# GpSimd's subtractions and products moved to VectorE in two stages, and a first score after 13 instead of 19 maximum units, in a fused attention, FFN and expert kernel

## The chip, the cores and the metric

The kernel runs on one core of a Trainium2 chip. A core has five engines that run side by side, each through its own queue in order: TensorE (PE, matrix multiply; PEld is its weight load), VectorE (DVE), ScalarE (ACT), GpSimd (POOL) and SyncE (SP, which here only issues DMAs). Engines wait for one another through semaphores. The metric is the device time of one execution in microseconds (us), the median of three runs.

## What is computed

Three stages, one after the other, all in 32-bit floats at the interface:

```python
# attention: q, k, v are (4, 8, 1152, 64); queries are averaged in pairs, so 576 queries
q_pool = q.reshape(B, H, S // 2, 2, D).mean(axis=3)
scores = q_pool @ k.T / sqrt(D)
attn = exp(scores - max(scores)); attn /= attn.sum() + 1e-9
x = attn @ v                       # 2304 tokens x 512
# dense FFN, w_in 512 x 2048, w_out 2048 x 512, given as 64-bit floats
h = x @ w_in;  x = (h * sigmoid(1.702 * h)) @ w_out
# experts: 8 experts, each token with a positive skip score goes to one
y = gate * (relu(x @ w1[e]) @ w2[e]);  out = x + y   # else out = x
```

## The kernel before, in words

Precision is kept by splitting each 32-bit operand of a matmul into a high part (F32R, written by a ScalarE copy) and a low part (operand minus high part), and by adding three products: high x high, low x high, high x low. Making low parts is elementwise work, and the change is largely about which engine does it.

**Attention** (`attention`) works on 16 pairs of heads; the two heads of a pair sit on partitions 0 to 63 and 64 to 127. A pair has 14 score units (`score_unit`): nine of 320 queries against 128 keys, then five of 256 queries against 256 or 128 keys. A unit's PSUM holds key x query scores, so the maximum of a query can't be subtracted per partition. Instead a fourth product adds it: `ONE` times `M2`, where row 0 and row 32 of each half of `M2` hold minus the maximum's high part `mh` and low part `ml`. So before a pair's first score can be finished, its maxima must be known: `max_unit` multiplies 128 queries by 384 keys at a time (two heads per unit, 14 units, 27 reductions by VectorE on line 230), `max_rows` takes the maximum over the three key parts, and `max_rows_put` transposes the result on TensorE, splits it and writes the rows into `M2` by small DMAs, all issued by SP. The loop runs in steps `g`; at step `g` it puts out score unit `g` and maximum unit `g + LEAD`, with `LEAD = 19`, so that 19 maximum units precede the first score unit. Loads, splits and sums of the following pairs hang on fixed steps (`BESIDE`, `start`, an agenda `ag`). VectorE, ScalarE and TensorE each run their list in the order in which the loop puts it out. Score tiles (`ss`) have two buffers, maximum tiles (`xs`, `mt`) three.

**FFN** (`ffn`): tokens come in chunks `CH` of 768, 384, 256, 256, 256 and 384, in pieces of at most 384, and the hidden dimension in 16 blocks `fb`. A step is one block and one piece: 12 matmuls of layer 1 into `h` (line 563, two buffers), `sigmoid` on ScalarE, product `g` on VectorE (569), high part `gh` on ScalarE, low part `gl` (572), and two steps later 9 matmuls of layer 2. In chunk 0, 32 steps long, each step also turns one 512-column piece of the 64-bit weights (`wr`) into two 32-bit parts with integer operations (`wsplit`): on VectorE a mask that drops the sign (450), a shift of the low word (451), a maximum (452), a shift-and-or (440), a shift-and-mask (454), an or (455) and a sign mask (444); ScalarE scales `t1` (441) and writes the high part (446); GpSimd multiplies the low part (445). The list `fq` holds these operations, and each step takes three ahead of `gl` and four behind it (`fill`). `put`, the high part of a piece, stands one step later in ScalarE's list, behind that step's line 441. The matmuls of block `fb` wait for the `wih` that `put` writes. GpSimd also makes `gl` in chunk 0 and multiplies the next chunk's tokens by their reciprocal sums (`xnorm`, 469).

**Experts** (`experts`): one slot for each expert that has tokens. A slot's tiles of 128 tokens run `tokens_tile`: `up` for the two halves of the hidden layer (24 matmuls, 922), relu of the first half on ScalarE (941) and of the second on VectorE (947), transposes (926), high and low parts `hT` (928, 929), `down` (24 matmuls, 937) and the result `yo` (957). Beside a slot's first tile the next expert's weights are split: 16 pieces (`splits`), high parts on ScalarE (800), low parts (801) on VectorE, every third (`q % 3 == 2`, five of 16) on GpSimd. They are put in lots of 3, 2, 2, 2 and 7 between the tile's own operations. As a stage buffer is released SP loads the weights of the expert after that (`weights`, eight DMAs of 512 KB). GpSimd also gathers token rows and scatters results by indirect DMAs.

Of the kernel before, what the change touches and what calls it, by code (L numbers as in the profile page):

```python
# [19 lines left out]
P = 128  # L20
# [51 lines left out]
class Kernel:  # L72
# [51 lines left out]
    def attention(self, ctx):  # L124
# [88 lines left out]
        def max_unit(p, i):  # L213
# [5 lines left out]
            if i < 12:  # L219
                part, t = divmod(i, 4)  # L220
                of = [(4 * u + t, part, d["qh"][HALF[u], t * P:t * P + P], d["kh"][HALF[u]]) for u in range(2)]
            else:
                of = [(8, part, BD[p % 2], d["kh"]) for part in ((0, 1), (2,))[i - 12]]
# [14 lines left out]
        def max_rows_put(p, m9):  # L238
# [6 lines left out]
            for row, m in ((0, mh), (32, ml)):  # L245
                for u in range(2):
                    r = slice(64 * u + row, 64 * u + row + 1)
                    dma(M2[p % 2][r, 0:512].rearrange("a (t q) -> a t q", q=P), m[4 * u:4 * u + 4])
                    dma(M2[p % 2][r, 512:], m[8:9, HALF[u]])
# [79 lines left out]
        LEAD = 19  # L329
# [35 lines left out]
        for g in range(-LEAD, NU * N + 20):  # L365
# [4 lines left out]
            px, ix = divmod(g + LEAD, NU)  # L370
            if 0 <= px < N:
                max_unit(px, ix)
                if ix == NU - 1:
                    max_rows(px)
# [9 lines left out]
            for f, *of in start.get(g + LEAD, ()):  # L384
                f(*of)
# [3 lines left out]
            if g == -LEAD + 12:  # L389
# [32 lines left out]
    def wsplit(self, fq, a, tmp, fb, k, ag=None):  # L422
# [20 lines left out]
        def last():  # L443
            V.tensor_scalar(sg, t2, 0xFF800000, None, op0=ALU.bitwise_and)
            (nc.gpsimd if fb else V).tensor_tensor(lo_t, t1.bitcast(F32), sg.bitcast(F32), op=ALU.mult)
            put = lambda: nc.scalar.activation(hi_t, t2.bitcast(F32), AF.Copy)  # L446
            put() if ag is None else ag.at(ag.now + 1, put)

        fq += [
            lambda: V.tensor_scalar(t2, hi, 0x7FFFFFFF, None, op0=ALU.bitwise_and),  # L450
            lambda: V.tensor_scalar(t1, hi, 23, None, op0=ALU.logical_shift_left),
            lambda: V.tensor_scalar(t2.bitcast(F32), t2.bitcast(F32), least, None, op0=ALU.max),
            low,
# [17 lines left out]
    def xtile(self, c, j, pc):  # L471
        i = (j * 2 + pc) if len(pieces(CH[c])) == 2 else (j * 2 + c % 2)
# [11 lines left out]
    def ffn(self, ctx):  # L484
# [60 lines left out]
        def xnorm(c, j, pc):  # L545
            xa[c, j, pc] = xr.tile([P, 384], F32, name="xa", tag="xa", bufs=4)
            self.xnorm(xa[c, j, pc], xraw.pop((c, j, pc)), c, j, pc, nc.gpsimd)
# [7 lines left out]
        def layer1(c, fb, pc, fa, fb_):  # L555
# [16 lines left out]
            (nc.gpsimd if c == 0 else V).tensor_tensor(gl, g, gh, op=ALU.subtract)  # L572
# [150 lines left out]
        for g in range(len(steps) + LAG):  # L723
            ag.now = g
            if g < len(steps):
# [11 lines left out]
                if fb == 0 and pc == 0 and c + 1 < len(CH):  # L737
                    for j in range(ND):
                        for q in range(len(pieces(CH[c + 1]))):
                            g0 = first[0, 10] + 2 * j if c == 0 else first[c, 4] + 2 * j  # L740
                            ag.at(g0, xload, c + 1, j, q)
                            ag.at(g0 + 1, xnorm, c + 1, j, q)
                            ag.at(first[c, NF - 1] + 1 if c == 0 else g0 + 4, xsplit, c + 1, j, q)
# [54 lines left out]
    def expert_split(self, s, q, raw, eng):  # L798
        hi, lo = self.piece(s, q)
        self.nc.scalar.activation(hi, raw, AF.Copy)  # L800
        eng.tensor_tensor(lo, raw, hi, op=ALU.subtract)  # L801
# [249 lines left out]
```

## Time and profile before

| | |
|---|---|
| median of 3 runs | 1119.11 us (1115.97 to 1127.57) |
| the profiled execution | 1114.21 us, of which its span, first to last instruction, is 1112.4 us |
| TensorE busy | 1017.9 us (91%) |
| VectorE busy | 806.9 us (73%) |
| GpSimd busy | 581.1 us (52%) |
| ScalarE busy | 482.1 us (43%) |
| granted TensorE clock, mean | 0.966 of 2.4 GHz |

A share over the whole span hides that the stages have different limits, so the stretches matter more: attention to 446 us, FFN chunk 0 to about 625 us, the other chunks to 912 us, experts to the end. In a timeline, a row is one instruction or a run of equal ones (`x27`): start, duration, engine, line, operation, output<-inputs; a bracket tells how long the engine had been idle and what ended that. Where two rows of one engine start closer together than the first one's duration, its pipeline overlaps them: the pace is read from start to start. The granted clock has two levels, 1.2 GHz (0.5) and 2.4 GHz (1.0); a mean between them is a mixture.

### The profile page before, as it was taken

To read this page: it belongs to the slowest core of one execution; us is meant where nothing else is said; L and a number is where in the kernel's file an instruction comes from. 1 tells how busy PE (TensorE), PEld (TensorE's weight loads), DVE (VectorE), ACT (ScalarE), POOL (GpSimd) and SP (SyncE) were. 2 spreads that over 40 slices of the span, in tenths; PEclk is the share of its full clock that TensorE was granted. 3 is DMA by queue.
4 is the path that set the end of the run, shared out by engine and by line. 5 is a ranking of instruction groups with operands and counts; after the bars stand their busy time and mean duration, and the time that the engine had idled before them with its cause. 6 is when DMAs were issued, how large, how long until landed. Compare 5 with 4: busy or idle time off the path is not lost. (4 is left out here: it accounts for less than half of the span.)

```text
span 1112.4 us, 19158 instructions
## 1 busy us (share of the span) xinstructions
PE 1017.9 (91%) x7002; PEld 801.3 (72%) x7002; DVE 806.9 (73%) x1584; ACT 482.1 (43%) x885; POOL 581.1 (52%) x408
## 2 busy tenths in 40 slices
PE   6999999999999999688978999999999989977893
PEld 4766767666776666587867898888889877755672
DVE  6767787778877772699999589787567555578734
ACT  2555555555555545243333332333332334256432
POOL 3698888998999988444445202101110106156413
PEclk9999999999999999889999999999999989988897
DMA  4233332223333210332333420211211326456301
GB/s 154 66 95 80 92 108 77 76 90 91 92 108 93 71 48 27 125 96 95 105 117 100 143 77 20 69 62 31 66 41 55 111 92 215 149 184 214 112 31 39
DMA packets 64325, 103.39 MB, mean 93 GB/s; under 512 B 18630, under 2 KB 34630, under 8 KB 64072
## 3 DMA queue, kind: packets, MB, share of 16 engines
q1 hardware_dynamic: 60148, 96.35, 27.4%
q0 software_dynamic: 3904, 5.15, 1.5%
q8 instruction: 69, 1.13, 0.4%
q14 instruction: 56, 0.46, 0.1%
q10 hardware_dynamic: 148, 0.30, 0.1%
HBM read 90.04 MB, written 17.35 MB: 97 GB/s over the span
## 5 line engine op out<-in xcount | busy, mean ns | idle before, releaser
L230 DVE TENSOR_REDUCE mx<-xs 128x1 f32<-128x384 f32 x432 | 213.0, 549 | 79.5 <-PE xs L227 74.8
L271 ACT ACTIVATE E<-ss 128x640 f32<-128x640 f32 (+1 forms) x224 | 174.0, 786 | 155.3 <-PE ss L270 123.0
L286 POOL TENSOR_TENSOR acc<-acc,E 128x640 f32<-128x640 f32 (+1 forms) x96 | 182.1, 1897 | 19.5 <-ACT E L271 15.4
L563 PE MATMUL h<-xh,wih 128*128 128x384 f32 (+1 forms) x448 | 145.8, 326 | 30.8 <-ACT wih L446 26.0
L306 PE MATMUL av<-E,v 128*64 128x256 f32 (+1 forms) x1152 | 157.1, 413 | 0.0
L563 PE MATMUL h<-xl,wih 128*128 128x384 f32 (+1 forms) x448 | 143.6, 321 | 0.7 <-DVE xl L482 0.6
L563 PE MATMUL h<-xh,wil 128*128 128x384 f32 (+1 forms) x448 | 143.2, 320 | 0.0
L563 PEld LDWEIGHTS h<-xh,wih 128*128 128x128 f32 x448 | 86.7, 194 | 43.0 <-ACT wih L446 31.7
L306 PEld LDWEIGHTS av<-E,v 128*64 128x64 f32 x1152 | 75.7, 136 | 56.0 <-issue 15.1
L587 PE MATMUL acc<-woh,gh 128*128 128x512 f32 x288 | 115.6, 401 | 0.0
L589 PE MATMUL acc<-woh,gl 128*128 128x512 f32 x288 | 115.2, 400 | 0.0
L588 PE MATMUL acc<-wol,gh 128*128 128x512 f32 x288 | 114.9, 399 | 0.0
L227 PE MATMUL xs<-kh,qh 64*128 64x384 f32 x384 | 102.3, 389 | 9.7 <-ACT kh L207 7.2
L270 PE MATMUL ss<-qh,kh 64*128 64x320 f32 (+1 forms) x576 | 107.1, 340 | 0.9 <-ACT E L271 0.9
L270 PE MATMUL ss<-M,ONE 64*128 64x320 f32 (+1 forms) x576 | 95.0, 296 | 2.5 <-DMA M<-ml 2.3
L569 DVE TENSOR_TENSOR g<-h,g 128x384 f32<-128x384 f32 (+1 forms) x112 | 55.8, 498 | 56.0 <-ACT g L568 51.3
L606 DVE CUSTOM_DVE_ANT_0 junk<-xs,wg 128x512 bf16<-128x512 f32 x135 | 94.7, 701 | 2.0
L658 POOL DMA_INDIRECT LIST<-pay,si x18 | 18.3, 1018 | 143.0 <-DVE si L655 75.6
L270 PE MATMUL ss<-qh,kl 64*128 64x320 f32 (+1 forms) x576 | 92.4, 294 | 0.0
L270 PE MATMUL ss<-ql,kh 64*128 64x320 f32 (+1 forms) x576 | 92.4, 294 | 0.0
L568 ACT ACTIVATE g<-h 128x384 f32<-128x384 f32 (+1 forms) x112 | 49.1, 439 | 99.1 <-PE h L563 98.8
L563 PEld LDWEIGHTS h<-xl,wih 128*128 128x128 f32 x448 | 87.0, 194 | 5.2 <-DVE xl L482 1.2
(196 smaller groups left out, 2176.8 us busy)
## 6 DMA issues: line engine op xcount, KB each, us to landing
stage<-w SPq DMA_DIRECT2D x40, 512.0 KB
qd<-qT SPq DMA_DIRECT2D x16, 576.0 KB
v<-v SPq DMA_DIRECT2D x16, 576.0 KB
kr<-kT SPq DMA_DIRECT2D x15, 576.0 KB
wr<-w_in SPq DMA_DIRECT2D x15, 512.0 KB
wr<-w_out SPq DMA_DIRECT2D x15, 512.0 KB
X<-xs SPq DMA_DIRECT2D x18, 256.0 KB
out<-xs SPq DMA_DIRECT2D x18, 256.0 KB
```

Source lines behind the costliest of these rows:

```text
L227: nc.tensor.matmul(ps[:, :384], q, k[:, part * 384:part * 384 + 384], start=True, stop=True)
L230: V.reduce_max(o, ps[:, :384], axis=AX.X)
L270: nc.tensor.matmul(ps[:, u, j * w:j * w + w], k[HALF[u]], q[HALF[u], qs], start=(n == 0), stop=(n == 3))
L271: nc.scalar.activation(place(p, i), ps[:, :, :len(kbs) * w], AF.Exp, scale=0.5 / D ** 0.5)
L286: G.tensor_tensor(d["a"], d["a"], place(p, i), op=ALU.add)
L306: nc.tensor.matmul(d["av"][HALF[u], :w], d["v"][:, u, kb], e[:, u, n * w:n * w + w], start=(kb == 0), stop=(kb == KB - 1))
L563: nc.tensor.matmul(h, a[:, d * P:d * P + P], x, start=(k == 0), stop=(k == 3 * ND - 1))
L569: V.tensor_tensor(g, h, g, op=ALU.mult)
L587: nc.tensor.matmul(acc[t], gh[:, ts], bh, start=(fb == 0), stop=False)
L588: nc.tensor.matmul(acc[t], gh[:, ts], bl, start=False, stop=False)
L589: nc.tensor.matmul(acc[t], gl[:, ts], bh, start=False, stop=(fb == NF - 1))
L606: V.tensor_tensor_reduce(out=junk, in0=R[grp[i]], in1=late["wg"][:, e], op0=ALU.mult, op1=ALU.add, scale=1.0, scalar=0.0, accum_out=R[grp] ...
```

## The change

Attention: 13 maximum units instead of 19 precede the first score. Pair 0 goes through the first three 128-query tiles with all their key parts before the fourth, takes their maxima at once and puts their rows into `M2` (`max_rows_first`), and puts the remaining rows later (`max_rows_second`); its `ml` rows are issued by ScalarE instead of SP. The six units left behind are made up two at a time on even steps. FFN chunk 0: `gl`, the weights' low product and chunk 1's `xnorm` go from GpSimd to VectorE, the sign-dropping mask from VectorE to ScalarE (`Abs`), the shift-and-or stands second instead of fourth. Chunk 1's tokens are loaded later and split a step sooner, into the buffers of piece 0. Experts: all 16 low parts on VectorE, the second relu on ScalarE.

```diff
-                part, t = divmod(i, 4)
+                part, t = divmod(i, 4) if p else (i // 3, i % 3) if i < 9 else (i - 9, 3)
+        def max_rows_first():
+            m9 = st[0]["m9"] = sm.tile([P, 9], F32, name="m9", tag="m9")
+            V.memset(m9, 0.0)
+            for u in range(2):
+                t = slice(4 * u, 4 * u + 3)
+                V.reduce_max(m9[:, t], st[0]["mx"][:, t], axis=AX.X)
+            max_rows_put(0, m9, (0, 3))
+        def max_rows_second():
+            m9 = sm.tile([P, 9], F32, name="m9", tag="m9")
+            V.reduce_max(m9, st[0]["mx"], axis=AX.X)
+            ag.at(ag.now + 1, max_rows_put, 0, m9, (3, 4))
-            for row, m in ((0, mh), (32, ml)):
+            for row, m, eng in ((0, mh, nc.sync), (32, ml, nc.sync if p else nc.scalar)):
-        LEAD = 19
+        LEAD, FIRST = 19, 13
-        for g in range(-LEAD, NU * N + 20):
+        m = 0
+        for g in range(-FIRST, NU * N + 20):
+            for _ in range(1 if g < 0 or m == g + LEAD or g % 2 else 2):
+                px, ix = divmod(m, NU)
+                if px < N:
+                    max_unit(px, ix)
+                    if px == 0 and ix == 8:
+                        max_rows_first()
+                    if ix == NU - 1:
+                        max_rows(px) if px else max_rows_second()
...
-            (nc.gpsimd if fb else V).tensor_tensor(lo_t, t1.bitcast(F32), sg.bitcast(F32), op=ALU.mult)
+            (nc.gpsimd if 0 < fb < EARLY else V).tensor_tensor(lo_t, t1.bitcast(F32), sg.bitcast(F32), op=ALU.mult)
+        nc.scalar.activation(t2.bitcast(F32), hi.bitcast(F32), AF.Abs)
-            lambda: V.tensor_scalar(t2, hi, 0x7FFFFFFF, None, op0=ALU.bitwise_and),
             lambda: V.tensor_scalar(t1, hi, 23, None, op0=ALU.logical_shift_left),
+            low,
             lambda: V.tensor_scalar(t2.bitcast(F32), t2.bitcast(F32), least, None, op0=ALU.max),
-            low,
...
-        i = (j * 2 + pc) if len(pieces(CH[c])) == 2 else (j * 2 + c % 2)
+        i = (j * 2 + pc) if len(pieces(CH[c])) == 2 else (j * 2 + (c + 1) % 2)
-            self.xnorm(xa[c, j, pc], xraw.pop((c, j, pc)), c, j, pc, nc.gpsimd)
+            self.xnorm(xa[c, j, pc], xraw.pop((c, j, pc)), c, j, pc, V if c == 1 else nc.gpsimd)
-            (nc.gpsimd if c == 0 else V).tensor_tensor(gl, g, gh, op=ALU.subtract)
+            V.tensor_tensor(gl, g, gh, op=ALU.subtract)
-                            g0 = first[0, 10] + 2 * j if c == 0 else first[c, 4] + 2 * j
+                            g0 = first[0, 12] + 2 * j - 1 if c == 0 else first[c, 4] + 2 * j
-                            ag.at(first[c, NF - 1] + 1 if c == 0 else g0 + 4, xsplit, c + 1, j, q)
+                            ag.at(first[c, NF - 1] if c == 0 else g0 + 4, xsplit, c + 1, j, q)
...
-                lambda q=q: self.expert_split(s, q, stage[q // 2][:, q % 2], nc.gpsimd if q % 3 == 2 else V)
+            return [lambda q=q: self.expert_split(s, q, stage[q // 2][:, q % 2]) for q in range(16)]
-            V.tensor_scalar(h[:, 512:], hp[1], 0.0, None, op0=ALU.max)
+            nc.scalar.activation(h[:, 512:], hp[1], AF.Relu)
```

`EARLY` is 1, so the condition `0 < fb < EARLY` never holds. With the added lines, line numbers of the changed kernel are some 20 higher.

How it moves VectorE's list in chunk 0, one step of it. Before, from one product `g` to the next (`t_6185` and `t_6184` are the weights' work tiles):

```order
L569 TENSOR_TENSOR g<-h,g 128x384
L450 TENSOR_SCALAR t_6185<-wr 128x512
L451 TENSOR_SCALAR t_6184<-wr 128x512
L452 TENSOR_SCALAR t_6185<-t_6185 128x512
L440 SCALAR_TENSOR_TENSOR t_6184<-wr,t_6184 128x512
L454 TENSOR_SCALAR t_6185<-t_6185 128x512
L455 SCALAR_TENSOR_TENSOR t_6185<-wr,t_6185 128x512
L444 TENSOR_SCALAR sg<-t_6185 128x512
```

The same step in the changed kernel:

```order
L593 TENSOR_TENSOR g<-h,g 128x384
L475 TENSOR_SCALAR t_6269<-wr 128x512
L464 SCALAR_TENSOR_TENSOR t_6269<-wr,t_6269 128x512
L477 TENSOR_SCALAR t_6270<-t_6270 128x512
L596 TENSOR_TENSOR gl<-g,gh 128x384
L478 TENSOR_SCALAR t_6270<-t_6270 128x512
L479 SCALAR_TENSOR_TENSOR t_6270<-wr,t_6270 128x512
L468 TENSOR_SCALAR sg<-t_6270 128x512
L469 TENSOR_TENSOR wol_6103<-t_6269,sg 128x512
```

The mask of line 450 has gone to ScalarE, the shift-and-or moved from fifth to third place, and `gl` and the low product are new here.

VectorE's list at attention's start, up to the second score step, before (`m_259` is the tile of the maxima):

```order
L230 TENSOR_REDUCE mx<-xs 128x1 x27
L235 TENSOR_REDUCE m_259<-mx 128x9
L230 TENSOR_REDUCE mx<-xs 128x1 x4
L243 TENSOR_SCALAR mh<-mt 9x128
L244 SCALAR_TENSOR_TENSOR ml<-mt,mh 9x128
L230 TENSOR_REDUCE mx<-xs 128x1 x16
```

And in the changed kernel:

```order
L231 TENSOR_REDUCE mx<-xs 128x1 x18
L242 MEMSET m_222 128x9
L245 TENSOR_REDUCE m_222<-mx 128x3 x2
L259 TENSOR_SCALAR mh<-mt 9x128
L260 SCALAR_TENSOR_TENSOR ml<-mt,mh 9x128
L231 TENSOR_REDUCE mx<-xs 128x1 x9
L250 TENSOR_REDUCE m_280<-mx 128x9
L231 TENSOR_REDUCE mx<-xs 128x1 x4
L259 TENSOR_SCALAR mh<-mt 9x128
L260 SCALAR_TENSOR_TENSOR ml<-mt,mh 9x128
```

The first rows now follow 18 reductions instead of 31, and a second pair of `mh` and `ml` comes 13 reductions later.

VectorE's list in an expert slot's first tile, from the first `hT` to the second, before:

```order
L929 TENSOR_TENSOR hT<-pq_10734,hT 128x512
L801 TENSOR_TENSOR wil_6051<-stage_10715,wih_6050 128x512
L947 TENSOR_SCALAR h<-hp_10733 128x512
L906 TENSOR_TENSOR xT_10707<-pt_10731,xT_10707 128x512
L801 TENSOR_TENSOR wol_6053<-stage_10715,woh_6052 128x512
L929 TENSOR_TENSOR hT<-pq_10735,hT 128x512
```

And in the changed kernel:

```order
L950 TENSOR_TENSOR hT<-pq_10748,hT 128x512
L825 TENSOR_TENSOR wol_6071<-stage_10728,woh_6070 128x512
L825 TENSOR_TENSOR wil_6065<-stage_10729,wih_6064 128x512
L927 TENSOR_TENSOR xT_10721<-pt_10745,xT_10721 128x512
L825 TENSOR_TENSOR wol_6067<-stage_10729,woh_6066 128x512
L825 TENSOR_TENSOR wil_6061<-stage_10730,wih_6060 128x512
L950 TENSOR_TENSOR hT<-pq_10749,hT 128x512
```

Two more low parts stand between the two, and the relu of the second half (`h`, line 947) is gone from this list.

## Rows read from the trace of the kernel before

**Rows 1.** Stages: us, busy of each engine (instructions), granted clock, DMA share, GB/s

```profile
29.38:446.00 416.62, 412.02 (x3978) 287.69 (x3975) 305.31 (x526) 232.68 (x369) 369.40 (x202) 1.00 0.27 81
474.00:570.50 96.50, 83.34 (x379) 72.77 (x379) 92.75 (x147) 37.00 (x73) 44.24 (x36) 0.93 0.32 102
616.60:912.00 295.40, 290.44 (x1674) 258.58 (x1674) 205.72 (x624) 101.76 (x238) 34.96 (x36) 1.00 0.22 72
912.00:1112.40 200.40, 157.01 (x684) 122.82 (x684) 121.48 (x151) 80.23 (x147) 85.74 (x77) 0.88 0.41 131
```

**Rows 2.** Waits of TensorE in 446 to 626 us: total, times, longest

```profile
PE h L563 <- ACT wih L446: 26.0, 13, 4.4
```

**Rows 3.** Timeline of VectorE, one step of chunk 0

```profile
474.33 0.56 DVE L569 TENSOR_TENSOR g<-h,g 128x384 f32<-128x384 f32 x1
474.80 1.12 DVE L450 TENSOR_SCALAR t<-wr 128x512 uint32<-128x512 uint32 x1
475.85 1.22 DVE L451 TENSOR_SCALAR t<-wr 128x512 uint32<-128x512 uint32 x1
...
479.67 0.56 DVE L569 TENSOR_TENSOR g<-h,g 128x384 f32<-128x384 f32 x1
```

**Rows 4.** Timeline of GpSimd in the same step

```profile
474.34 1.30 POOL L445 TENSOR_TENSOR wol<-t,sg 128x512 fp32r<-128x512 f32 x1 [2.89 <-ACT g L568]
475.60 1.19 POOL L572 TENSOR_TENSOR gl<-g,gh 128x384 fp32r<-128x384 f32 x1
```

**Rows 5.** Timeline of VectorE, the first weight split, with GpSimd idle

```profile
454.91 0.43 DVE L450 TENSOR_SCALAR t<-wr 128x512 uint32<-128x512 uint32 x1 [11.84 <-DMA wr<-w_in]
455.25 0.42 DVE L451 TENSOR_SCALAR t<-wr 128x512 uint32<-128x512 uint32 x1
455.58 0.42 DVE L452 TENSOR_SCALAR t<-t 128x512 f32<-128x512 f32 x1
455.92 0.68 DVE L440 SCALAR_TENSOR_TENSOR t<-wr,t 128x512 uint32<-128x512 uint32 x1
456.52 0.42 DVE L454 TENSOR_SCALAR t<-t 128x512 uint32<-128x512 uint32 x1
456.97 0.69 DVE L455 SCALAR_TENSOR_TENSOR t<-wr,t 128x512 uint32<-128x512 uint32 x1
457.70 0.43 DVE L444 TENSOR_SCALAR sg<-t 128x512 uint32<-128x512 uint32 x1
```

**Rows 6.** Groups by line and shape, whole span: busy us, mean ns, idle before

```profile
L572 DVE TENSOR_TENSOR gl<-g,gh 128x384 fp32r<-128x384 f32 x32 | 18.3, 571 | 6.5 <-ACT gh L570 6.5
```

**Rows 7.** Timeline of VectorE in an expert slot

```profile
981.16 7.21 DVE L801 TENSOR_TENSOR wol<-stage,woh 128x512 fp32r<-128x512 f32 x1
...
988.89 0.68 DVE L801 TENSOR_TENSOR wol<-stage,woh 128x512 fp32r<-128x512 f32 x1
989.49 0.68 DVE L801 TENSOR_TENSOR wil<-stage,wih 128x512 fp32r<-128x512 f32 x1
```

**Rows 8.** Timeline of GpSimd in that slot, first and last of five such rows

```profile
981.63 1.31 POOL L801 TENSOR_TENSOR wil<-stage,wih 128x512 fp32r<-128x512 f32 x1
...
986.57 1.25 POOL L801 TENSOR_TENSOR wil<-stage,wih 128x512 fp32r<-128x512 f32 x1
```

**Rows 9.** Waits of TensorE in 912 to 1112 us: total, times, longest

```profile
PE y L937 <- DVE hT L929: 17.1, 4, 6.0
PE pq L926 <- DVE h L947: 5.3, 2, 3.6
```

**Rows 10.** One slot with a single tile, columns as in rows 1

```profile
994.44:1014.74 20.30, 16.11 (x64) 12.57 (x65) 16.64 (x17) 11.30 (x22) 11.54 (x10) 0.83 0.69 230
```

**Rows 11.** Timeline of attention's start, VectorE, SP and ScalarE

```profile
7.92 12.73 DVE L230 TENSOR_REDUCE mx<-xs 128x1 f32<-128x384 f32 x27 [2.46 <-PE xs L227]
...
25.72 2.40 SPq L83 DMA_DIRECT2D M<-ml  x4
...
29.38 0.70 ACT L271 ACTIVATE E<-ss 128x640 f32<-128x640 f32 x1 [13.49 <-PE ss L270]
```

More of the change, by code (lines that the diff above doesn't have):

```diff
@@ L236, in max_rows, with max_rows_put @@
             ag.at(ag.now + 2, max_rows_put, p, m9)
-        def max_rows_put(p, m9):
+        def max_rows_first():
[9 more added lines that the diff above has]
+            ag.at(ag.now + 1, max_rows_put, 0, m9, (3, 4))
+        def max_rows_put(p, m9, of=(0, 4)):
+            a, b = of
             ps = mxp.tile([P, 512], F32, name="mt", tag="mx")
@@ L244, in max_rows_put @@
             V.scalar_tensor_tensor(ml, ps[0:9, 0:P], -1.0, mh, op0=ALU.mult, op1=ALU.subtract)
-            for row, m in ((0, mh), (32, ml)):
+            for row, m, eng in ((0, mh, nc.sync), (32, ml, nc.sync if p else nc.scalar)):
                 for u in range(2):
                     r = slice(64 * u + row, 64 * u + row + 1)
-                    dma(M2[p % 2][r, 0:512].rearrange("a (t q) -> a t q", q=P), m[4 * u:4 * u + 4])
-                    dma(M2[p % 2][r, 512:], m[8:9, HALF[u]])
+                    to = M2[p % 2][r, a * P:b * P].rearrange("a (t q) -> a t q", q=P)
+                    eng.dma_start(to.bitcast(F32), m[4 * u + a:4 * u + b].bitcast(F32))
+                    if b == 4:
+                        eng.dma_start(M2[p % 2][r, 512:].bitcast(F32), m[8:9, HALF[u]].bitcast(F32))
         def place(p, i):
@@ L369, in attention @@
                 score_unit(p, i)
[L370 to L374, printed above, removed]
+            for _ in range(1 if g < 0 or m == g + LEAD or g % 2 else 2):
[6 more added lines that the diff above has]
+                        max_rows(px) if px else max_rows_second()
+                for f, *of in start.get(m, ()):
+                    f(*of)
+                m += 1
             pa, ia = divmod(g - 2, NU)
@@ L383, in attention @@
                 sum_unit(p, i)
-            for f, *of in start.get(g + LEAD, ()):
-                f(*of)
             for step, f, ahead, *of in BESIDE:
@@ L388, in attention @@
                     f(p + ahead, *of)
-            if g == -LEAD + 12:
+            if g == 0:
                 empty_lists()
@@ L796, in piece, with expert_split @@
         return self.W[fb, ("wih", "woh")[k]], self.W[fb, ("wil", "wol")[k]]
[L798 removed]
+    def expert_split(self, s, q, raw):
         hi, lo = self.piece(s, q)
         self.nc.scalar.activation(hi, raw, AF.Copy)
[L801 removed]
+        self.nc.vector.tensor_tensor(lo, raw, hi, op=ALU.subtract)
     def first_expert_load(self, m):
@@ L811, in first_expert_split @@
         for c in range(2):
-            self.expert_split(0, 2 * m + c, self.first[:, m % 4 * 2 + c], self.nc.vector)
+            self.expert_split(0, 2 * m + c, self.first[:, m % 4 * 2 + c])
         if m < 4:
@@ L892, in splits @@
         def splits(s):
-            return [
-                lambda q=q: self.expert_split(s, q, stage[q // 2][:, q % 2], nc.gpsimd if q % 3 == 2 else V)
-                for q in range(16)
-            ]
+            return [lambda q=q: self.expert_split(s, q, stage[q // 2][:, q % 2]) for q in range(16)]
         def xpose(t):
```

## The prediction

> **What bounds the kernel now.** I read the stretches first, because the change touches three of them and the whole-span shares mix their limits. In attention after its start TensorE is busy 412.02 of 416.62 us, and in the FFN's later chunks 290.44 of 295.40 us [rows 1]: there TensorE sets the time, and work taken off other engines is worth nothing. In FFN chunk 0 VectorE is busy 92.75 of 96.5 us and TensorE 83.34 [rows 1]; TensorE's waits, 26.0 us in 13 turns, end with ScalarE's `wih` [rows 2], which stands behind ScalarE's line 441 and so behind VectorE's line 440. Chunk 0 runs at VectorE's pace, 5.34 us a step (474.33 to 479.67 [rows 3]). In the experts no engine is full (TensorE 157.01 of 200.40 us), and TensorE's waits name VectorE: 17.1 us for `hT`, 5.3 us for the second relu [rows 9].
>
> Then I asked why VectorE is late. The same two operations, lines 450 and 451, take 1.12 and 1.22 us in a step [rows 3] and 0.43 and 0.42 us when GpSimd is idle [rows 5]; in the step GpSimd runs its product and its subtraction at just those moments, 474.34 to 476.79 [rows 4]. In the experts one subtraction on VectorE lasts 7.21 us [rows 7] while GpSimd runs five of its own back to back, 981.63 to 987.82 [rows 8]; an undisturbed one next to it lasts 0.68 us. So GpSimd's elementwise work costs VectorE about its own length, on VectorE's critical list.
>
> **FFN chunk 0.** From start to start, undisturbed [rows 5]: shift 0.33 us, maximum 0.34, shift-and-or 0.60, shift-and-mask 0.45, or 0.73, sign mask 0.46 (0.43 and the 0.03 seen between dependent rows). The shift-and-or now follows its own input directly; I add 0.12, the difference that a dependent mask shows (0.45 against 0.33). Together 3.03. The product `g` takes 0.47 [rows 3]. New on VectorE are `gl`, 0.571 us long [rows 6] and some 0.1 less from start to start, 0.47, and the low product, which I price like an expert subtraction of the same shape, 0.60 [rows 7]. Sum 4.57 us a step against 5.34. TensorE is close behind: 83.34 us of work in these 18 steps are 4.63 a step, at a granted clock of 0.93 [rows 1]. I take 4.6, a saving of 0.74. From 474 us to the last block's start at 616.6 us there are 26 such steps: 19 us. Chunk 1's `xnorm` adds four operations of 0.47 to VectorE, 2 us, but those four took GpSimd's time, and so VectorE's, before; I count them as even. At chunk 0's start TensorE waited longest, 4.4 us [rows 2]; with the shift-and-or third instead of fifth in a step, `wih` comes about 2 us earlier once, and three more steps are shorter: 5 us. In all 24 us. ScalarE gains the mask: it is busy 37.00 of 96.5 us [rows 1], room for 18 times some 0.6 us, an estimate from VectorE's 0.60 for the same width. Nothing waits for it, since it stands ahead of the step's sigmoid and its weights were loaded two steps before; without that cover, each late load would hold the sigmoid. The order of instructions shows no further table load on ScalarE. Bounds: if the two new operations cost VectorE what they cost GpSimd (1.30 and 1.19 [rows 4]), the step is 5.99 and the stretch loses 17 us; at VectorE's measured paces and a TensorE at full clock it gains 28.
>
> **Experts.** The waits of rows 9, 22.4 us, go. After a wait TensorE's clock has fallen: in a slot with one tile the granted clock is 0.83 [rows 10], 3.5 us of full-speed time in 20.30 us. There are four such slots and a cold start after one; part of that loss lies in the wait itself, so I count 8 us. Against it: VectorE's list between the two `hT` holds two more subtractions (0.60 us each [rows 7]) and one relu less, and seven subtractions instead of five stand before `yo`. TensorE has 12 matmuls and at least 8 transposes to do between the two, which hides most; I take 2 us off. ScalarE takes the relu, 11.30 us busy of 20.30 [rows 10]. 28 us. Bounds: 33 if no wait is left, 8 if the long VectorE rows have another cause.
>
> What is late next is the weights. A one-tile slot would shrink from 20.3 to about 14 us, and it moves 230 GB/s times 20.3 us, 4.7 MB [rows 10]. That is 335 GB/s. No row here shows that rate sustained. The eight loads can use the whole slot and the first half of the next, so I assume they fit.
>
> **Attention's start.** 27 reductions take 12.73 us, 0.47 each, from 7.92 us [rows 11]. The first rows now follow 18 of them and not 31: 13 fewer, 6.1 us. SP issued eight row DMAs one after the other, the last four in 2.40 us [rows 11], 0.60 each; now two on SP lie beside two on ScalarE, six fewer in a row: 3.6 us. Against it, eight matmuls for maxima still precede the first score and wait for VectorE's tiles, about five reductions, 2.4 us. The first exponential, at 29.38 us [rows 11], should come about 7 us sooner. Six units, 12 reductions or 5.6 us of VectorE, are made up during the first ten steps, and ScalarE's second `ml` issue holds two exponentials until VectorE delivers. I keep 5 us. From then on TensorE sets the pace and carries the gain to the end. Bounds: 7 if the catching up hides, minus 2 if it is paid in full and ScalarE's wait (four issues of 0.60) besides.
>
> **Sum.** 5 + 24 + 28 = 57 us. The profiled execution took 1114.21 us, 1.8 more than its span; less 57 is 1057. The median of the runs is 4.9 us above it, 1062. I predict 1060.
>
> **Rivals.** (1) The experts become bound by the weights. If loads sustain only 230 GB/s [rows 10], the three one-tile slots that follow each other keep their 20.3 us instead of some 14, and 18 of the 28 us are lost: 1078. For it: no faster rate is in my rows. Against it: the loads waited for stage buffers that a held-up VectorE released late. (2) The long VectorE row is not GpSimd's doing but some other wait; then only 8 us come from the experts: 1080. The page "SBUF — State Buffer" of the Trainium skill (Who interferes with whom) says that VectorE and GpSimd hold their shared pair for a whole instruction and that "Issue order, not op shape, decides who blocks". By it VectorE, which started at 981.16 ahead of GpSimd's 981.63, would not have lost 6 us to five instructions. The row disagrees with the order but agrees with the overlap, which ends 0.55 us after the fifth. Chunk 0 has no such doubt. (3) Attention's catching up eats its gain: 1065 to 1067, inside my range. (4) The other side: VectorE becomes the bound. If the moved operations cost what they cost on GpSimd, chunk 0's step is 5.99 us and its 31 steps lose 20 us; an expert's 16 subtractions at 1.31 us are 21 us, more than a one-tile slot of 20.3, so the experts gain nothing. With 5 us from the start: about 1134. It decides as soon as the two operations together exceed 1.84 us (5.34 less the 3.50 that stay) on VectorE; 0.571 [rows 6] and 0.68 [rows 7], both VectorE's own, stand against it.
>
> **Chances.** Forecast 0.74, rival 1 0.12, rival 2 0.06, rival 3 0.06, rival 4 0.02. The range is 1042 to 1082: below, both bounds of 28 and 33 us reached and the start's 7 in full (68 off 1114 is 1046, and a little for terms left out); above, rivals 1 and 2. A measurement of this kernel tells about 1% from no change. Only rival 4 and a failure of two terms at once end there or beyond: faster 0.97, within 1% 0.01, slower 0.02.
>
> **What would show it.** In the changed profile a chunk-0 step on VectorE should repeat every 4.5 to 4.7 us, with the shift near 0.42 and no row above 0.75; the expert stretch should hold no VectorE row of 7 us and no TensorE wait above 2 us; the first exponential should start near 22 us and pair 1's first 5 us sooner. I am wrong if the step stays above 5 us, if TensorE's waits in the experts move to DMA or ScalarE, or if the first exponential comes early and pair 1's does not.

## The result and the profile after

The changed kernel takes 1080.4 us (median of four runs, 1079.35 to 1082.4), the old one 1120.48 (1115.97 to 1127.57): a ratio of 0.9639, 95% interval 0.9585 to 0.9693. Faster, as forecast, and 1080.4 lies in the range; but it is 20 us above the 1060 predicted, and only just inside, so the working is to be judged by its terms. The profiled execution took 1079.35 us with a span of 1077.5, 34.9 below the old one's 1112.4. Two single runs in a slow state, at granted clocks of 0.56 and 0.66, are left out of all that follows: 1575 us of the old kernel, run beside the variants, and 1369 us of e11.

First where it went, cut at the same instructions in both traces. The stretches and the differences are worked out from the starts of the first exponentials of pair 0 and pair 1, attention's last exponential and the matmul that adds up the experts' counts (`cn`).

| stretch | before | after | difference | forecast |
|---|---|---|---|---|
| start of the span to pair 1's first exponential | 53.87 | 59.77 | +5.9 | -5 |
| to attention's last exponential | 387.2 | 387.8 | +0.6 | 0 |
| to `cn` (the FFN) | 469.05 | 447.58 | -21.5 | -24 |
| to the end (the experts) | 202.3 | 182.35 | -20.0 | -28 |

So one term of the forecast has the wrong sign, one (28 for 20) is two fifths too large, and one is nearly right. The windows of the changed kernel (columns as in [rows 1]) show each stage; the last is one slot with a single tile:

```profile
23.63:59.77 36.14, 32.78 (x249) 21.46 (x251) 22.86 (x48) 13.46 (x22) 19.31 (x11) 0.91 0.12 35
59.77:452.00 392.23, 387.24 (x3745) 269.33 (x3741) 283.79 (x491) 220.31 (x350) 349.29 (x192) 1.00 0.27 81
471.00:570.50 99.50, 91.68 (x447) 79.27 (x445) 95.03 (x194) 58.39 (x107) 0.00 (x0) 1.00 0.36 116
895.20:1077.50 182.30, 151.09 (x695) 118.54 (x694) 99.39 (x179) 85.37 (x158) 46.86 (x47) 0.92 0.44 144
990.65:1008.56 17.91, 14.65 (x64) 11.44 (x65) 13.04 (x21) 11.64 (x23) 5.25 (x6) 0.92 0.77 266
```

In chunk 0 (third line) GpSimd is silent, VectorE still full (95.03 of 99.5 us), and TensorE's granted clock is 1.00, the 2.4 GHz level, instead of 0.93. The experts before, cut at the same instruction:

```profile
910.10:1112.40 202.30, 158.45 (x695) 123.78 (x694) 122.91 (x160) 80.50 (x147) 85.74 (x77) 0.88 0.40 130
```

For the same 695 matmuls TensorE is busy 151.09 us instead of 158.45, at a granted clock of 0.92 instead of 0.88: the clock gave back 7.4 us, close to the 8 that I counted. Its idle time fell from 43.9 to 31.2 us, 12.6 and not the 20.4 that I counted. Between pair 1 and the end of attention nothing moved: what the start loses is carried to the end.

A step of chunk 0 on VectorE, to be held against [rows 3]:

```profile
498.84 0.55 DVE L593 TENSOR_TENSOR g<-h,g 128x384 f32<-128x384 f32 x1
499.31 0.42 DVE L475 TENSOR_SCALAR t<-wr 128x512 uint32<-128x512 uint32 x1
499.76 0.69 DVE L464 SCALAR_TENSOR_TENSOR t<-wr,t 128x512 uint32<-128x512 uint32 x1
500.37 0.42 DVE L477 TENSOR_SCALAR t<-t 128x512 f32<-128x512 f32 x1
500.70 0.55 DVE L596 TENSOR_TENSOR gl<-g,gh 128x384 fp32r<-128x384 f32 x1
...
502.88 0.69 DVE L469 TENSOR_TENSOR wil<-t,sg 128x512 fp32r<-128x512 f32 x1
503.49 0.55 DVE L593 TENSOR_TENSOR g<-h,g 128x384 f32<-128x384 f32 x1
```

From `g` to `g` it is 4.65 us (forecast 4.57 to 4.6), the shift takes 0.42 instead of 1.22, no row of the step exceeds 0.75, and both operations that came over from GpSimd cost what I had priced.

Attention's start on ScalarE, to be held against [rows 11]:

```profile
23.63 0.70 ACT L289 ACTIVATE E<-ss 128x640 f32<-128x640 f32 x1 [2.40 <-PE ss L288]
25.94 0.70 ACT L289 ACTIVATE E<-ss 128x640 f32<-128x640 f32 x1 [1.60 <-PE ss L288]
27.80 0.59 ACTq L265 DMA_DIRECT2D M<-ml  x1
28.43 0.60 ACTq L267 DMA_DIRECT2D M<-ml  x1
29.07 0.60 ACTq L265 DMA_DIRECT2D M<-ml  x1
29.71 0.60 ACTq L267 DMA_DIRECT2D M<-ml  x1
30.36 0.70 ACT L289 ACTIVATE E<-ss 128x640 f32<-128x640 f32 x1 [3.72 <-DMA M<-ml]
...
38.52 0.71 ACT L289 ACTIVATE E<-ss 128x640 f32<-128x640 f32 x1 [4.19 <-PE ss L288]
...
59.77 1.41 ACT L289 ACTIVATE E<-ss 128x640 f32<-128x640 f32 x2 [4.44 <-PE xs L228]
```

The first exponential comes 5.75 us sooner (7 were forecast); the sixth (38.52) is already later than the old kernel's (37.0), and pair 1's first is 5.9 later. Between the second and the third ScalarE is held for 3.72 us: first it waits for VectorE's `ml`, then it issues four small DMAs of 0.60 us each. Behind that the granted clock in 31 to 45 us is 0.76:

```profile
31.00:45.00 14.00, 13.22 (x80) 7.72 (x80) 8.23 (x16) 6.38 (x13) 7.01 (x5) 0.76 0.05 7
```

TensorE's waits in the experts, to be held against [rows 9]:

```profile
PE hp L943 <- PEq L1028: 9.8, 5, 3.4
PE pt L922 <- DMA xg<-X,ids: 3.5, 1, 3.5
...
PE y L958 <- DVE hT L950: 0.4, 1, 0.4
```

and one of them before:

```profile
PE hp L922 <- PEq L1007: 4.3, 5, 1.5
```

The 22.4 us for `hT` and the relu are 0.4. A wait at the start of a slot, behind the `If` of line 1028 (1007 before), has grown from 4.3 to 9.8 us, the wait for gathered token rows (`xg`) from 1.8 to 3.5 us, and the three slots with one tile that follow each other take 15.86, 16.74 and 17.91 us where I had forecast about 14.

What that wait is can be read from the row of the branch itself, in the sequencer that feeds TensorE (in ns the shortest, median and longest; then the start in us). One such row of the changed kernel, and one of the old:

```profile
L1028 PEldq COMPARE_BRANCH  x1: 4936/4936/4936, 985.1 to 985.1; - x1
L1007 PEldq COMPARE_BRANCH  x1: 4520/4520/4520, 1009.6 to 1009.6; - x1
```

The three branches between the one-tile slots of the changed kernel last 3.63, 4.94 and 4.86 us. The sequencer runs ahead of the matmuls: each branch begins 2.2 us before the slot's last matmul ends, and the next slot's first matmul starts 0.6 us behind the branch. So TensorE stands for 2.03, 3.36 and 3.26 us. The old kernel's branches last as long (4.37, 4.52 and 4.36 us), but its last matmuls ran in part at the lower clock (0.43 us from start to start instead of 0.23) and covered 3.5 to 4.5 us, so that 0.6 to 1.5 us were left. In every trace of this case a 16 KB packet of a DMA queue that the profile calls `instruction` ends 1.1 to 1.6 us before such a branch does; I take it that the code behind the jump is being loaded. No run here does without the branch, so that reading is not tested.

### The profile page after: what moved, and what is told of

It is laid out like the page before. It is cut to its first block, busy times and chain, and to the rows that moved or that the text cites. A ratio compares the mean times of both kernels' runs of the same rounds, so it can differ in the third digit from the quotient of the medians.

```text
span 1077.5 us, 19084 instructions
## 1 busy us (share of the span) xinstructions
PE 1005.2 (93%) x7003; PEld 787.7 (73%) x7003; DVE 759.6 (70%) x1642; ACT 508.3 (47%) x928; POOL 462.7 (43%) x312
## 3 DMA queue, kind: packets, MB, share of 16 engines
q0 software_dynamic: 3904, 5.15, 1.6%
## 5 line engine op out<-in xcount | busy, mean ns | idle before, releaser
L304 POOL TENSOR_TENSOR acc<-acc,E 128x640 f32<-128x640 f32 (+1 forms) x96 | 182.9, 1905 | 26.6 <-ACT E L289 22.7
L587 PE MATMUL h<-xh,wih 128*128 128x384 f32 (+1 forms) x448 | 143.1, 319 | 17.6 <-ACT wih L470 11.4
L587 PE MATMUL h<-xl,wih 128*128 128x384 f32 (+1 forms) x448 | 140.8, 314 | 0.2
L587 PE MATMUL h<-xh,wil 128*128 128x384 f32 (+1 forms) x448 | 140.5, 314 | 0.0
L493 POOL TENSOR_TENSOR xa<-xraw 128x256 f32<-128x256 f32 (+1 forms) x16 | 15.2, 951 | 263.7 <-DMA xraw<-RD 258.5
L594 ACT ACTIVATE gh<-g 128x384 fp32r<-128x384 f32 (+1 forms) x112 | 53.7, 480 | 102.6 <-DVE g L593 102.6
```

The lines of the kernel that those rows point to most:

```text
L304: G.tensor_tensor(d["a"], d["a"], place(p, i), op=ALU.add)
L587: nc.tensor.matmul(h, a[:, d * P:d * P + P], x, start=(k == 0), stop=(k == 3 * ND - 1))
L594: nc.scalar.activation(gh, g, AF.Copy)
```

## The experiments

All are the changed kernel with the edit shown; times are medians of four runs, to be compared with 1080.4. The old kernel, run beside them, gave medians of 1115 to 1122 and single runs from 1101 to 1130, so its spread is wider than most differences here, and I compare the variants with one another.

### Attention's start

**e1, start undone.** The whole of attention is the old one:

```diff
-        LEAD, FIRST = 19, 13
+        LEAD = 19
...
-            for row, m, eng in ((0, mh, nc.sync), (32, ml, nc.sync if p else nc.scalar)):
+            for row, m in ((0, mh), (32, ml)):
...
```

> The changed kernel (1080.4 us) with attention's part of the change taken back: one set of rows on SP, 19 units ahead of the first score. Theory A (the new start costs: after the change pair 1's first exponential comes at 59.8 us, 5.9 later than before, and pair 15's last one 6.6 later): the last exponential of attention comes at 441 instead of 447.6 us and the time is 1074, 6 below the changed kernel. Rival B (my forecast's: the early start is worth 5 us, and the later attention is a difference between two executions): 1085. Rival C (whatever the start gains or loses is evened out behind it): 1080 within 1.

Measured: 1073.43 us (1071.83 to 1074.97). Pair 1's first exponential is back at 53.93. Theory A: the new start costs 7 us, and no run of either kernel reaches into the other's spread.

**e2, second rows from SP.**

```diff
-            for row, m, eng in ((0, mh, nc.sync), (32, ml, nc.sync if p else nc.scalar)):
+            for row, m, eng in ((0, mh, nc.sync), (32, ml, nc.sync if p or b == 4 else nc.scalar)):
```

> The changed kernel, but the second, small set of rows of ml goes from SP again, so that ScalarE issues only the first set, before its first exponential. Theory A (the loss lies in ScalarE's four held issues, 27.80 to 30.31 us, which make TensorE wait and its clock fall to half from 30.94 to 37.76): no stretch at half clock there, the fourth exponential some 3 us sooner, pair 1's first exponential at 56 to 57 instead of 59.8 us, time 1077. Rival B (the loss is the catching up, two units of maxima in each second step, on VectorE and TensorE): pair 1's first exponential stays within 1 us of 59.8, time 1080.

Measured: 1078.75 us (1076.59 to 1081.16), which overlaps the changed kernel's runs, so the trace has to decide. The clock stays at its upper level in 31 to 45 us,

```profile
31.00:45.00 14.00, 13.62 (x113) 8.59 (x109) 10.91 (x22) 6.01 (x11) 10.26 (x6) 1.00 0.17 45
```

the fourth exponential comes at 30.5 instead of 32.1 (half of what I expected), and pair 1's first at 56.54, within the 56 to 57 of theory A. So ScalarE's issues account for 3.2 of the 5.9 us; whether the rest is the catching up is for e10 to show.

**e10, nothing to catch up.** The maxima of the first part still come ahead and from two queues, but 19 units precede the first score:

```diff
-        LEAD, FIRST = 19, 13
+        LEAD, FIRST = 19, 19
```

> The changed kernel with one number changed: the first score stands 19 units of maxima behind the first, as in the old kernel, instead of 13, so that nothing is to be made up. The maxima of pair 0's first part still come ahead, with their own rows, from two queues. Theory A (behind the first exponential TensorE has no free time, so each of the twelve made-up maxima costs it about 0.36 us or more, besides ScalarE's held issues): the first exponential at 26.5 to 28.5 us, no wait of TensorE for rows ahead of it above 0.5, pair 1's first exponential at 51.5 to 52.5 instead of 59.8, time 1071 to 1073. Rival B (the split rows themselves, a second transposition and second set of issues, cost what is lost): pair 1's first exponential at 55 or later, time 1075 or more.

Measured: 1071.83 us (1070.66 to 1073.66), 8.6 below the changed kernel and the best of all. The timeline of ScalarE in e10:

```profile
25.92 0.60 ACTq L267 DMA_DIRECT2D M<-ml  x1
28.15 0.70 ACT L289 ACTIVATE E<-ss 128x640 f32<-128x640 f32 x1 [6.67 <-PE ss L288]
...
52.57 1.38 ACT L289 ACTIVATE E<-ss 128x640 f32<-128x640 f32 x2 [3.36 <-PE ss L288]
```

The issues now lie ahead of the first exponential, where ScalarE has nothing else to do, and TensorE waits for no row. Against e2 (24.20 and 56.54) the first exponential comes 3.95 us later and pair 1's 3.97 us sooner. So six units ahead of the first score cost 0.66 us each; made up behind it, they cost 7.92 / 6 = 1.32 us each. From the first exponential to pair 1's first, TensorE in e2 and in e10:

```profile
24.20:56.54 32.34, 30.43 (x249) 20.39 (x251) 22.78 (x48) 13.45 (x22) 19.30 (x11) 1.00 0.13 38
28.15:52.57 24.42, 24.42 (x235) 18.19 (x235) 17.95 (x33) 13.46 (x21) 17.27 (x9) 1.00 0.23 70
```

In e10 it is busy without a gap. Of e2's 7.92 us, 6.0 are work and 1.9 idle time (0.7 for the rows, 1.1 for VectorE's maxima): behind the first exponential TensorE has no time to give away.

**e6, old order, two queues.** e1 with pair 0's `ml` rows on ScalarE:

```diff
-            for row, m in ((0, mh), (32, ml)):
+            for row, m, eng in ((0, mh, nc.sync), (32, ml, nc.sync if p else nc.scalar)):
```

> The kernel of e1 (old start, new rest, 1073.4 us) with one thing of the new start kept: pair 0's four rows of ml are issued on ScalarE instead of behind mh's four on SP; the maxima stay 19 units ahead. Theory A (TensorE has no free time behind the first exponential, so the moved maxima cost it their own time; only the waits for rows before the first exponential, 1.37 and 0.62 us, can be won): first exponential at 27.5 to 28 instead of 29.6, pair 1's first 1.5 to 2 us before 53.9, time 1071.5. Rival B (ScalarE's issuing costs as much as it saves, as behind the first exponential): pair 1's first exponential at 53.9 or later, 1073 to 1075.

Measured: 1074.51 us (1071.15 to 1079.14). In the trace the first exponential comes at 28.11, pair 1's at 52.36, 1.6 before e1's, as theory A has it; but the time is not the 1071.5 of theory A, it lies where rival B put it and can't be told from e1. Inconclusive in time, confirmed in the trace; and there all that e10 (52.57) has over e1 is the second queue.

### FFN chunk 0

**e8, chunk 0 undone.** The old `wsplit`, the low product and `gl` on GpSimd, the old places of `xnorm`:

```diff
...
-        nc.scalar.activation(t2.bitcast(F32), hi.bitcast(F32), AF.Abs)
...
+            lambda: V.tensor_scalar(t2, hi, 0x7FFFFFFF, None, op0=ALU.bitwise_and),
...
-            V.tensor_tensor(gl, g, gh, op=ALU.subtract)
+            (nc.gpsimd if c == 0 else V).tensor_tensor(gl, g, gh, op=ALU.subtract)
...
```

> The changed kernel with the whole of chunk 0's part taken back (the split's order, its mask on VectorE, the low product and gl on GpSimd, chunk 1's xnorm on GpSimd and its times); start and experts stay as changed. If the part is worth what the two traces show between attention's last exponential and the counts (469.05 less 447.58): 1080.4 + 21.5 = 1102. If my forecast's 24 us: 1104. If it is worth hardly more than gl alone (14.6 by e3): 1095 to 1097.

Measured: 1103.09 us (1097.9 to 1108.94, ten runs): the part is worth 22.7 us, between the trace's 21.5 and my 24.

**e3, only `gl` back on GpSimd.**

```diff
-            V.tensor_tensor(gl, g, gh, op=ALU.subtract)
+            (nc.gpsimd if c == 0 else V).tensor_tensor(gl, g, gh, op=ALU.subtract)
```

> The changed kernel with one operation back on GpSimd: the subtraction gl in chunk 0; the weights' low product and the new order of the split stay. Theory A (VectorE cannot run beside GpSimd, so GpSimd's operation costs VectorE about its own length): VectorE's list loses 0.47 us and gains up to 1.2, the rows next to gl last up to 1.2 us instead of 0.43, chunk 0's step goes from 4.66 to between 5.0 and 5.4 us, and over 31 steps the time rises by 10 to 22 us, to 1091 to 1102. Rival B (the long rows have another cause, and GpSimd's work lies beside VectorE's): no row gets longer, VectorE's step is shorter by 0.47 and TensorE's 4.63 us sets it: 1079 to 1080.

Measured: 1095.03 us (1093.94 to 1099.17), 14.6 more, in theory A's range. VectorE in e3:

```profile
491.72 0.42 DVE L475 TENSOR_SCALAR t<-wr 128x512 uint32<-128x512 uint32 x1
492.17 0.69 DVE L464 SCALAR_TENSOR_TENSOR t<-wr,t 128x512 uint32<-128x512 uint32 x1
492.78 1.25 DVE L477 TENSOR_SCALAR t<-t 128x512 f32<-128x512 f32 x1
494.06 0.43 DVE L478 TENSOR_SCALAR t<-t 128x512 uint32<-128x512 uint32 x1
```

and GpSimd:

```profile
492.44 1.30 POOL L596 TENSOR_TENSOR gl<-g,gh 128x384 fp32r<-128x384 f32 x1 [3.83 <-ACT gh L594]
```

The operation that was under way when GpSimd began (492.17) keeps its 0.69; the next (492.78) lasts 1.25 instead of 0.42 and ends 0.29 behind GpSimd's end. From start to start it takes 1.28 instead of 0.33, so taking 0.47 off VectorE's list put 0.95 on it: a step takes 5.15 us instead of 4.65 (501.95 to 507.10, from `g` to `g`), and 31 steps of 0.48 more are 14.9, against the 14.6 measured. This is a clean case: one operation, one long row of 1.22 to 1.25 us, in every step but the first. What the low product, the mask and the new order are worth one by one of the other 8 us was not tried. The Trainium skill ("SBUF — State Buffer", Who interferes with whom) says that the pair shared by VectorE and GpSimd is held for a whole instruction by whoever issued first; this row agrees, at 1.25 against 0.42 us.

### The experts

**e4, five low parts back on GpSimd.**

```diff
-            return [lambda q=q: self.expert_split(s, q, stage[q // 2][:, q % 2]) for q in range(16)]
+            return [lambda q=q: self.expert_split(s, q, stage[q // 2][:, q % 2], nc.gpsimd if q % 3 == 2 else V) for q in range(16)]
```

> The changed kernel with every third of an expert's 16 low parts (five of them) back on GpSimd; the second relu stays on ScalarE. Theory A (five GpSimd subtractions in a row shut VectorE out): VectorE rows of 5 to 7 us are back in each slot, TensorE waits for hT again, and the experts' 182.35 us become 195 to 202: 1093 to 1100. Rival B (in the old kernel the second relu on VectorE, not the low parts, held TensorE): no change or a gain of up to 3 us for each one-tile slot, since VectorE's list, which now ends last, is five subtractions shorter: 1070 to 1080.

Measured: 1088.54 us (1084.79 to 1097.74), 8 more by the medians, less than theory A's 13 to 20, but clear of rival B. The profiled execution is the slowest of the four, 9 us above the median: in it the experts take 194.9 instead of 182.35 us, and the stages before them, which the edit doesn't touch, 5.9 more. VectorE's long rows are back, six of 6.0 to 6.9 us, and TensorE waits 11.9 us for `hT`. VectorE in e4:

```profile
999.12 6.90 DVE L825 TENSOR_TENSOR wil<-stage,wih 128x512 fp32r<-128x512 f32 x1 [0.19 <-ACT wih L824]
```

GpSimd:

```profile
999.23 1.31 POOL L825 TENSOR_TENSOR wil<-stage,wih 128x512 fp32r<-128x512 f32 x1
...
1004.18 1.28 POOL L825 TENSOR_TENSOR wil<-stage,wih 128x512 fp32r<-128x512 f32 x1
```

VectorE's row starts 0.11 us ahead of five GpSimd rows and ends 0.56 behind the last. Here the Trainium skill's rule of issue order does not fit: by it the first to start would have gone through, and whichever came first, one instruction would have waited for one other and not for five.

**e11, second relu back on VectorE.**

```diff
-            nc.scalar.activation(h[:, 512:], hp[1], AF.Relu)
+            V.tensor_scalar(h[:, 512:], hp[1], 0.0, None, op0=ALU.max)
```

> The changed kernel with the second relu of an expert tile back on VectorE (all low parts stay there too). Theory A (in one-tile slots VectorE's list is what lasts, 0.6 us longer now, and TensorE's wait for that relu was GpSimd's doing): time 1081 to 1083, no wait of TensorE for h above 1 us. Rival B (the 5.3 us for the second relu were VectorE's own queue, low parts in front of the relu): TensorE waits for h 3 us and more in all, time 1085 to 1088. Rival C: no difference, 1080.

Measured: 1083.01 us (median of three runs, 1080.58 to 1083.7), 2.6 more, which overlaps the changed kernel's runs; by the time theory A can't be told from rival C. But TensorE does not wait for `h`, and waits 1.5 us for `hT`, so rival B falls: the old kernel's 5.3 us for the second relu were GpSimd's doing, not the relu's.

**e5, a larger first lot.**

```diff
-A0, A1, A2, A3 = 3, 2, 2, 2
+A0, A1, A2, A3 = 6, 2, 2, 2
```

> The changed kernel with one number changed: the first lot of an expert's splits is six instead of three, and the last lot four instead of seven. Theory A (a one-tile slot now lasts as long as VectorE's list: SP issues each weight load when a low part is done, and the next slot begins behind SP's last load; VectorE's idle 1.71 and 3.44 us behind the third low part are lost because ScalarE's fourth split waits behind the first relu): VectorE has no such gap, the three one-tile slots of 15.86, 16.74 and 17.91 us fall to 14.2 to 15, and the time is 1073 to 1076. Rival B (my prediction's rival 1: the weights' rate, 266 to 292 GB/s in these slots, sets their length): slots and time stay, 1080. Rival C (the first relu now waits behind three more splits, 1.6 us, and TensorE waits for it): slots longer by about 1 us, 1083 to 1086.

Measured: 1080.52 us (1076.9 to 1084.04), no change; my theory A missed. VectorE's gap moved from behind the third low part to behind the sixth (2.58 and 1.89 us in the first two slots), and at the start of a slot VectorE came late:

```profile
975.88 0.69 DVE L825 TENSOR_TENSOR wil<-stage,wih 128x512 fp32r<-128x512 f32 x1 [3.53 <-DMA stage<-w]
```

The profile puts the 3.53 us, and 2.08 in the next slot, down to the weights, but the starts of the rows tell of another wait. At every change out of one of these slots, in every trace, ScalarE's first split starts 0.07 us behind the signal that TensorE gives after its branch, and in e5 VectorE's first low part follows 0.66 us later (975.15, 975.22 and 975.88 here). It is TensorE's branch, 5.66 us long here, that all of them wait for. The three slots take 17.42, 18.22 and 18.09 us.

**e7, half the weight bytes.** From the third expert loaded on, the second half of each row of the weights is left out, and the splits and products run on what else stands in the stage:

```diff
-                dma(t, src)
+                dma(t if s == 1 else t[:, :, :256], src if s == 1 else src[:, :, :256])
```

> The changed kernel with half of the weight bytes from the third expert loaded on: each load of an expert's stage brings the first 256 of 512 columns of each row, and the splits and products run on what else stands in the stage. Everything else is the same. Theory A (the list of VectorE, not the weights, sets a one-tile slot): slots stay at 15.5 to 18 us, time 1079 to 1081, the rate about halves. Rival B (the weights set it): the one-tile slots fall to 13 to 14 us, time 1070 or less.

Measured: 1078.77 us (1077.67 to 1081.49); the slots take 16.27, 15.42 and 18.13 us at 129 to 153 GB/s, 49.8 in sum against 50.5. The weights' rate does not set the changed kernel's slots.

**e9, e5 and e7 together**, with the same half of the weights left out.

> e5 (first lot of six) with the halved weight loads of e7; the same half of the weights is left out as there. e5's VectorE waited 3.53 and 2.08 us for a stage's load in two one-tile slots, and e7 by itself was not faster. Theory A (two limits lie close together: VectorE's list, and behind it the weights' rate; each alone hides the other): with both eased the one-tile slots fall to 14 to 15 us, and the time is 1071 to 1075. Rival B (a slot's length hangs on neither, for instance on TensorE at half clock behind its wait for the slot's start): 1078 to 1081 as in e5 and e7.

Measured: 1079.2 us (1075.53 to 1080.21). The slots take 15.61, 15.68 and 17.15 us, 48.4 in sum against 50.5: 2 us less at most, so the weights are not what is left. VectorE's gap behind the sixth low part still stood, which e12 takes away.

**e12, e9 with a first lot of ten**, the same half of the weights left out.

```diff
-A0, A1, A2, A3 = 6, 2, 2, 2
+A0, A1, A2, A3 = 10, 1, 1, 1
```

> e9 (halved weight loads; the same half of the weights is left out) with a first lot of ten splits, then one, one, one and three, instead of six, two, two, two and four. In e9 the three one-tile slots still took 15.61, 15.68 and 17.15 us, and VectorE stood idle in each for about 1.9 us behind its sixth low part, because ScalarE's seventh split waits behind the first relu, which TensorE at half clock delivers late. Theory A (that order on ScalarE is the rest of the slot beyond VectorE's twenty operations of 0.60 us and the 1.7 us between two slots): the gap goes and the slots take 13.8 to 14.5 us, time 1073 to 1076. Rival B (TensorE, at half clock behind its wait for the slot's start, or the hand-over from slot to slot, is the limit by itself): slots 15 us or more, time 1078 to 1080.

Measured: 1081.71 us (1077.58 to 1082.49): rival B by the slots, though the median is 2 us above its 1078 to 1080. VectorE's low parts now end early (990.05, ahead of TensorE's last matmul, which ends at 991.04), and the slots still take 16.62, 16.78 and 17.20 us. VectorE in e12:

```profile
989.37 0.68 DVE L825 TENSOR_TENSOR wol<-stage,woh 128x512 fp32r<-128x512 f32 x1
991.08 0.75 DVE L978 SCALAR_TENSOR_TENSOR yo<-y,ids,x_e 128x512 f32<-128x512 f32 x1 [1.03 <-PE y L958]
```

and TensorE:

```profile
990.65 0.39 PE L958 MATMUL y<-woh,hT 128*128 128x512 f32 x1
993.04 0.49 PE L943 MATMUL hp<-wih,xT 128*128 128x512 f32 x1 [2.00 <-PEq L1028]
```

and the windows of the three slots:

```profile
959.64:976.26 16.62, 13.46 (x64) 10.47 (x65) 13.28 (x22) 11.71 (x23) 10.16 (x6) 1.00 0.49 148
976.26:993.04 16.78, 14.77 (x64) 11.69 (x65) 13.13 (x21) 11.63 (x23) 6.49 (x5) 0.90 0.49 147
993.04:1010.24 17.20, 14.76 (x64) 11.70 (x65) 13.13 (x21) 11.69 (x23) 6.30 (x6) 0.90 0.49 153
```

TensorE's own work in such a slot is 13.4 us at full clock (first line), without a gap above 1 us. Then it stands for 2.22, 2.00 and 2.44 us at its branch, 3.7 to 4.1 us long here; VectorE has finished `yo` 1.2 to 1.7 us before TensorE goes on (in the changed kernel once 0.2 us after), so `yo` is not what it waits for. In the second and third slot the clock falls behind the stop (granted 0.90), which costs another 1.3. That is the slot: 13.4 + 2.0 + 1.3 = 16.7 for the second. In e5, e7, e9, e12 and the changed kernel each of the three slots is TensorE's busy time and its stop to within 0.1 us, but for e12's first, where it also waits 0.9 us for a relu. Neither VectorE's list, 13.1 us, nor the weights (all transfers together 200 to 292 GB/s in the changed kernel) sets a slot, which is why easing one, or both, moved next to nothing.

## Why the prediction was right, and where it was off

**What bounds it, and GpSimd as the cause: right.** The reading of [rows 3 to 5, 7, 8], that GpSimd's work costs VectorE about its own length, is what e3 (0.95 us on the list for a row of 1.30) and e4 (a row of 6.90 us beside five that fill 6.23) show. Rival 2 (another cause of the long rows) falls: the rows come back with GpSimd's five subtractions and with nothing else. Rival 4 (VectorE the bound, slower) falls too: the moved operations last 0.55 and 0.69 us.

**Chunk 0: right, 3 us too large.** The step is 4.65 us for a forecast of 4.6. The 26 steps that I counted, from product `g` to product `g`, run from 474.33 [rows 3] and 479.77 to these:

```profile
616.91 0.56 DVE L569 TENSOR_TENSOR g<-h,g 128x384 f32<-128x384 f32 x1
602.66 0.55 DVE L593 TENSOR_TENSOR g<-h,g 128x384 f32<-128x384 f32 x1
```

That is 142.6 us before (first row) and 122.9 after: 19.7 for the 19. `xnorm`, which I counted as even, helped: a step with it took 6.2 us before and takes 5.1 now. The term that was mis-sized is the start of chunk 0, "5 us". From attention's last exponential to the first of these steps it is 33.3 us before and 32.2 after, so it came out at 1.1; another 1.1 came in the steps behind, of which 0.5 was lost again up to `cn`. My upper bound of 28 does not come out of its terms: 26 times 0.77 and 5 are 25.

**Experts: mechanism right, size off by 8 us.** The waits of [rows 9] went (22.4 to 0.4), and the clock's 8 us came as 7.4. The step that failed is "A one-tile slot would shrink from 20.3 to about 14 us": it left out that TensorE stands at its own branch at each change of slot. That wait was 4.3 us in all in the old kernel, because the branch, which was as long, lay beside matmuls that ran in part at the lower clock. Now it is 9.8 us: 5.5 of the 22 came back there, 1.7 in the wait for gathered rows, and the other 2 or so in gaps too small for the view of waits; 2 of these 9 I had taken off beforehand. Rival 1 (the weights) had the result, about 1078, but not the reason: e7 took half of the weights away and won 1.6 us, within the spread of the runs.

**Attention's start: wrong in sign, 11 us.** Two steps failed. The first is "I keep 5 us", which let the six units be made up beside other work. The reason against it stood in my own first sentence: in attention TensorE is busy 412.02 of 416.62 us [rows 1], so anything moved behind the first score is paid in TensorE's time. By e2 and e10 that is 7.9 us for the six units, against 3.95 won ahead: a loss of 4.0. The second is ScalarE's second `ml` issue, priced at four times 0.60 as a bound and otherwise as harmless: with what TensorE waited behind it and the clock that it lost there it cost 3.2 us (e2). Against the two stands the second queue, which by itself brings pair 1 forward by 1.6 us (e6 against e1). Rival 3 stopped at "eats its gain"; the lower bound of minus 2 was too narrow for the two together, 5.9. What I named as a sign of being wrong, a first exponential that comes early and a pair 1 that does not, is just what the trace showed.

**The sum.** 57 forecast, 34.9 by the two profiled executions: 11 lost at the start, 8 in the experts, 2.5 in chunk 0 and 0.6 within attention. By the medians the gain is 40; the old kernel's runs scatter by some 2%, and its profiled execution lies 6.3 us below their median, the changed kernel's 1.05. That 1080.4 still lies in the range is luck: its upper end was drawn for rivals 1 and 2, and neither is what happened.

The best version run is e10, 1071.83 us: it keeps the two later stages and the two queues and drops only the early start.

## What to carry to other kernels

Before work is moved out of a ramp, look at the engine that bounds the stretch behind it: an early start is worth nothing if what was skipped has to be made up where that engine has no free time. When a large wait inside a repeated section goes, add up what one repetition still has to pass one after the other, the branch at its end included, and not only the list of the busiest engine. A wait that a view puts down to the last signal seen is checked by the starts of the rows around it. And one operation taken off a full engine onto a neighbour that holds it up can cost that engine more than it did itself (0.95 for 0.47 us here).

## What was not expected of the hardware

- A small DMA issued on ScalarE holds its list for 0.60 us, and the issue waits there for its data: four of them behind the second exponential held ScalarE for 3.72 us, and the granted clock of 31 to 45 us fell to 0.76. The same four ahead of the first exponential (e10) leave TensorE without a wait.
- Five GpSimd subtractions that follow each other let a VectorE row that started 0.11 us before the first of them end only behind the last, after 6.90 us, while a single one makes one row 0.83 us longer (e4, e3).
- TensorE's branch out of a slot lasts 3.6 to 4.9 us in the changed kernel and shows in the view of waits only with the 2.0 to 3.4 us that its last matmuls don't cover. The three one-tile slots take 50.5 us with it, and 53.7, 49.8, 48.4 and 50.6 with VectorE's order, the weights or both eased (e5, e7, e9, e12).
